# Feed-forward weight loads issued by SyncE in place of GpSimd, in a forward and backward kernel of one decode block

## The chip, the cores and the metric

The kernel runs on one core of a Trainium2 chip. The metric is device time in microseconds (us) of one execution. The kernel before was run three times: median 599.85 us, from 598.75 to 599.95. One further execution was recorded by the hardware profiler; it took 598.03 us, of which the profile shows a span of 596.2 us.

The core has five engines with their own instruction streams: TensorE (PE, with its weight loads PEld), VectorE (DVE), ScalarE (ACT), GpSimd (POOL) and SyncE (SP). A transfer between the chip's main memory and the on-chip memory is a DMA. An engine issues it and goes on; 16 DMA engines carry it out. DMAs issued by GpSimd go through queue q0 (its descriptors are written by software on GpSimd), those issued by SyncE through queue q1 (descriptors made by hardware). Instructions of one engine start in order: one that waits holds up all behind it on the same engine.

## The reference

One token with a model width of D = 1024 goes through a block of attention and a gated feed-forward layer, each with a layer norm that is scaled and shifted by a condition vector. The outputs are the result and the gradients of all inputs but one. Cut to what matters here:

```python
def _A_ref(x, k_cache, v_cache, wq, wo):       # attention over the last 4096 cache rows
    ...
def _B_ref(x, w_gate, w_up, w_down):           # D = 1024, F = 3584
    g = jnp.einsum('bsd,df->bsf', x, w_gate)
    u = jnp.einsum('bsd,df->bsf', x, w_up)
    h = _sigmoid(g) * u
    return jnp.einsum('bsf,fd->bsd', h, w_down)

mod = (_silu(c) @ w_mod).reshape(c.shape[0], 6, 1, -1)
h = _layernorm(x) * (1 + ca) + sa
x = x + ga * _A_ref(h, ...)
h = _layernorm(x) * (1 + cb) + sb
x = x + gb * _B_ref(h, ...)
_out, _vjp = jax.vjp(_f, A_x, A_k_cache, ...)  # and the gradients of grad_out
return (_out0, *grads)
```

There is one token, so each weight is used for one matrix-vector product forward and one backward, and its gradient is an outer product of two vectors, as large as the weight itself. The gradients of the two caches have 65,536 rows per head, of which all but the last 4,096 are zero; those zeros must be written too. That makes the kernel a mover of bytes: 60.30 MB are read from main memory and 185.60 MB are written.

## The kernel before

The stages follow each other: modulation vectors and query (to about 60 us), attention, a folding of the output projection into blocks (to about 300 us, TensorE work with `b_ps`), the feed-forward layer forward and backward in one sweep (about 310 to 480 us), and the remaining gradients (to the end). The instruction order on each engine is the order in which the program writes it; there is no planner.

Zeros are written by `zero(n)`: each call issues n fills of 1 MB on GpSimd (line 169; the "narrow" ones by lines 162 and 165). Their numbers at each point are given by hand in lists; for the feed-forward blocks this is `Z_FFN[q]`, four numbers for four places in a block, (1, 0, 0, 2) for blocks 0 to 4.

The feed-forward layer is cut into NB = 7 blocks of 512 columns of gate and up and 512 rows of down. A block's gate and up weights take 2 MB of the on-chip array `arena`, in one of two buffers (`q % 2`); each half (`j0` = 0 or 4, four groups of 128 rows of D) of each is a DMA of 512 KB, with four runs of 512 bf16 values (1 KB) in each partition. `load_ug` (line 863, its DMAs on line 865) loads, `store_ug` (line 867, DMAs on 869) stores the gradients, which are written over the weights in place. Down's weights have one buffer of 1 MB in two halves, loaded by `load_wd` (line 852) and stored by `store_wd` (line 855), both on SyncE, with one run of 4 KB per partition.

In the loop, iteration q does the following.

- Backward of block q: eight times a reduction on VectorE (`ttr`, line 210) over a weight slice and then its outer product, on ScalarE for the first five (line 241) and on VectorE for the other three (line 206), into the same bytes. After the fourth, `store_ug(q, 0, 4)` and `zero(z[0])`; after the eighth, `store_ug(q, 4, 4)` and `zero(z[1])`.
- Forward of block q + 1: `front` (64 products of 128 x 128 weight pieces on TensorE, line 954), `gates` (two sigmoids on ScalarE, line 959), `hh_ops` on VectorE, then in two halves `ffn_mm` (TensorE, line 971), `wd_ttr` and `wd_outer` (VectorE; `wd_outer` ends with `store_wd`), and `dug_part`, which prepares the vector for the next backward sweep.
- In between, `side()` runs transposes that later stages need, on TensorE and ScalarE.
- Loads of block q + 2 into the buffer that block q has left: `load_ug(q + 2, 0, 4)` after the first `wd_ttr`, `load_ug(q + 2, 4, 4)` after the second `wd_outer`, `zero(z[3])` behind it, and last `load_wd`.

A load waits until the stores of the same bytes have landed. All stores, fills and gate and up loads stand in GpSimd's one stream. The loads of blocks 0 and 1 are issued ahead of the loop.

Of the kernel before, what the change touches and what calls it, by code (L numbers as in the profile page):

```python
# [23 lines left out]
NB = F // FB  # L24
# [34 lines left out]
def kernel(  # L59
# [26 lines left out]
    nc = tc.nc  # L86
# [60 lines left out]
    def dep(later, earlier):  # L147
        tc.add_manual_dep(later.ins, earlier.ins.name,
                          mybir.DependencyInfo(mybir.DependencyClass.Sync, mybir.DependencyReason.DATA),
                          reason="pace")  # L150

    def zero(n, after=None):
        for _ in range(n):
            if len(zleft) <= keep[0]:
                return
            region, narrow_ = zleft.pop(0)
            first = None
            if narrow_:
                nc.gpsimd.inc_swdge_sem([], [], mode="reset_dge_cursor")  # L160
                n = nlen - ncount.pop()
                first = nc.gpsimd.dma_start(
                    out=rest[0:NS, 0:nlen * 128].rearrange("p (t x) -> p t x", t=2)[:, :, n * 64:(n + 1) * 64],
                    in_=zeros[0:NS, 0:64].rearrange("p (t x) -> p t x", t=1).broadcast_to([NS, 2, 64]))
                ins = nc.gpsimd.dma_start(
                    out=region[8:P, :].bitcast(FP32).rearrange("(t p) x -> p t x", t=2),
                    in_=zeros[0:60, :].rearrange("p (t x) -> p t x", t=1).broadcast_to([60, 2, ZW // 2]))
            else:
                ins = nc.gpsimd.dma_start(out=region.bitcast(FP32), in_=zeros[:, :])  # L169
            if after is not None:  # L170
                dep(first or ins, after)
# [26 lines left out]
    def addv(out, a, b):  # L198
        return tt(out, a, b, ALU.add)

    def cp(out, a):
        return nc.vector.tensor_copy(out=out, in_=a)  # L202
# [6 lines left out]
    def ttr(out, w, b, acc):  # L209
        return nc.vector.tensor_tensor_reduce(out=out, in0=w, in1=b, scale=1.0, scalar=0.0,  # L210
                                              op0=ALU.mult, op1=ALU.add, accum_out=acc)
# [233 lines left out]
    def side(n=1):  # L445
        for _ in range(n):
            if jobs:
                jobs.pop(0)()
# [402 lines left out]
    def load_wd(q, s):  # L851
        nc.sync.dma_start(out=wd_v[:, 2 * s:2 * s + 2, :], in_=wd_dram(B_w_down, q, s))
# [4 lines left out]
    def ug_part(view, q, j0, n):  # L857
        return view[:, j0:j0 + n, q * FB:(q + 1) * FB]

    def ug_tile(q, k, j0, n):  # L860
        return ug_v[:, q % 2, j0 // 4, j0 % 4:j0 % 4 + n, k, :]

    def load_ug(q, j0, n):
        for k, view in ((0, wu_view), (1, wg_view)):
            nc.gpsimd.dma_start(out=ug_tile(q, k, j0, n), in_=ug_part(view, q, j0, n))  # L865

    def store_ug(q, j0, n):
        for k, view in ((0, dwu_view), (1, dwg_view)):
            nc.gpsimd.dma_start(out=ug_part(view, q, j0, n), in_=ug_tile(q, k, j0, n))  # L869
# [20 lines left out]
    mod_tiles(md_ps, sb_t, range(4), True)  # L890
    wm_sec(5, 0, 4, 48)
    load_ug(0, 0, 4)
    load_ug(0, 4, 4)
    park(2, pna, "na")
    park(3, pna, "na")
# [29 lines left out]
    zero(Z_FOLD[0])  # L925
    park(4, ppq, "pq")
    load_ug(1, 0, 4)
    load_ug(1, 4, 4)
    zero(Z_FOLD[1])
# [18 lines left out]
    def front(q):  # L948
        gu = gu_t[q % 2]
        for col, k in ((4, 0), (0, 1)):  # L950
            for i in range(4):
                f0 = 256 * (i // 2) + i % 2
                for j in range(KD):
                    nc.tensor.matmul(gu[:, col + i:col + i + 1], lhsT=ug_v[:, q % 2, j // 4, j % 4, k, f0:f0 + 255:2],  # L954
                                     rhs=h2_bf[:, j:j + 1], start=(j == 0), stop=(j == KD - 1))

    def gates(q):
        r, gu = small[q % 2], gu_t[q % 2]
        nc.scalar.activation(out=r["sg"], in_=gu[:, 0:4], func=ACT.Sigmoid)
        nc.scalar.activation(out=r["om"], in_=gu[:, 0:4], func=ACT.Sigmoid, scale=-1.0)  # L960

    def hh_ops(q):
        r, up = small[q % 2], gu_t[q % 2][:, 4:8]
        mulv(r["hh_bf"], r["sg"], up)
        mulv(r["hh"], r["sg"], up)
        mulv(r["hom"], r["hh"], r["om"])

    def ffn_mm(q, s):
        for i in (2 * s, 2 * s + 1):
            for k in range(KD):  # L970
                nc.tensor.matmul(ffn_ps[:, k:k + 1], lhsT=wd_v[:, i, k * P:(k + 1) * P],
                                 rhs=small[q % 2]["hh_bf"][:, i:i + 1], start=(i == 0 and k == 0),
                                 stop=(i == 3), skip_group_check=True)

    def wd_ttr(q, s):
        for i in (2 * s, 2 * s + 1):
            ttr(junk, wd_v[:, i, :], b1k, small[q % 2]["dhh"][:, i:i + 1])

    def wd_outer(q, s):
        for i in (2 * s, 2 * s + 1):  # L980
            outer_dve(wd_v[:, i, :], small[q % 2]["hh"][:, i:i + 1], b1k)
        store_wd(q, s)

    def dug_part(q):
        r = small[q % 2]
        mulv(r["dug_bf"][:, 0:4], r["dhh"], r["sg"])
        mulv(r["dug_bf"][:, 4:8], r["dhh"], r["hom"])
        tp = new_tp("tp_dug")
        for i in range(8):
            nc.tensor.transpose(tp[:, i * P:(i + 1) * P], r["dug_bf"][:, i:i + 1].broadcast_to([P, P]), ident_bf[:, :])  # L990
        nc.scalar.copy(out=dug_b.rearrange("p (s f j) -> p s f j", s=4, j=2),  # L991
                       in_=tp.rearrange("p (s j f) -> p s f j", s=4, j=2))
# [6 lines left out]
    def unpark(p):  # L999
        nc.scalar.copy(out=B_home[p], in_=BT_ps[p][:, :])  # L1000
# [16 lines left out]
    for q in range(NB):  # L1017
        z = Z_FFN[q]
        more = q + 1 < NB
        for j in range(KD):  # L1020
            w = ug_v[:, q % 2, j // 4, j % 4, :, :].rearrange("p k f -> p (k f)")
            ttr(w, w, dug_b, dh2acc[:, q * KD + j:q * KD + j + 1])
            if not more and j in (3, 5, 6):
                unpark({3: 2, 5: 0, 6: 4}[j])
            (outer_act if j < 5 else outer_dve)(w, h2[:, j:j + 1], dug_b)
            if more and 0 < j < 5:
                side()
            if j == 0:
                if q == 0:
                    cp(ffn, ffn_ps)  # L1030
                else:
                    addv(ffn, ffn, ffn_ps)
            if j == 3:
                store_ug(q, 0, 4)
                zero(z[0])
        store_ug(q, 4, 4)
        zero(z[1])
        if more:
            front(q + 1)
            gates(q + 1)  # L1040
            side()
            hh_ops(q + 1)
            ffn_mm(q + 1, 0)
            wd_ttr(q + 1, 0)
            if q + 2 < NB:
                load_ug(q + 2, 0, 4)
            wd_outer(q + 1, 0)
            zero(z[2])
            side()
            ffn_mm(q + 1, 1)  # L1050
            wd_ttr(q + 1, 1)
            side()
            dug_part(q + 1)
            wd_outer(q + 1, 1)
            if q + 2 < NB:
                load_ug(q + 2, 4, 4)
            zero(z[3])
            if q + 2 < NB:
                load_wd(q + 2, 0)
                load_wd(q + 2, 1)  # L1060
        else:
            zero(z[2] + z[3])
# [270 lines left out]
```

## Time and profile before

| What | Value |
|---|---|
| Median of three runs | 599.85 us |
| The profiled execution's own time | 598.03 us |
| Its span in the profile | 596.2 us |
| Busy: TensorE / VectorE / ScalarE / GpSimd | 69% / 57% / 45% / 27% of the span |
| Moved by DMA | 246.63 MB, mean 414 GB/s |
| Zero fills of 1 MB | 114, median 16.2 us from issue to landing |
| Up and gate loads of 512 KB | 14 each, 9.4 and 9.6 us from issue to landing |
| Down loads and SyncE's stores of 512 KB | 14 and 20, 8.9 and 9.2 us |

How to read it: a page of the profile cuts the span into 40 slices of 14.9 us. In the row "DMA" a 9 means that the 16 engines had packets for 90% of the time or more; the row below gives GB/s. A table by window gives, for a stretch of the span, the busy time of each engine with its number of instructions, the granted TensorE clock, the DMA share (it can be over 1, as packets of two queues overlap in the records) and GB/s. A timeline row gives start, duration, engine, line, operation, what is written and read, and in brackets the idle time before and what ended it. A row of waits gives who waited for what: microseconds in total, how often, and the longest. Each transfer is carried out in packets, and the trace records start, size and duration of each packet and its queue.

### The profile page before, as it was taken

To read this page: it belongs to the slowest core of one execution; us is meant where nothing else is said; L and a number is where in the kernel's file an instruction comes from. 1 tells how busy PE (TensorE), PEld (TensorE's weight loads), DVE (VectorE), ACT (ScalarE), POOL (GpSimd) and SP (SyncE) were. 2 spreads that over 40 slices of the span, in tenths; PEclk is the share of its full clock that TensorE was granted. 3 is DMA by queue.
4 is the path that set the end of the run, shared out by engine and by line. 5 is a ranking of instruction groups with operands and counts; after the bars stand their busy time and mean duration, and the time that the engine had idled before them with its cause. 6 is when DMAs were issued, how large, how long until landed. Compare 5 with 4: busy or idle time off the path is not lost.

```text
span 596.2 us, 11043 instructions
## 1 busy us (share of the span) xinstructions
PE 409.2 (69%) x4587; PEld 275.6 (46%) x4612; DVE 337.7 (57%) x641; ACT 266.0 (45%) x408; POOL 159.4 (27%) x253
## 2 busy tenths in 40 slices
PE   3997688999999989999975436445445086774220
PEld 3995334334344545546654425434334066574220
DVE  3654499999511010070007587896787887858360
ACT  2589514567211014212224565773765835883110
POOL 3113123222222122222222224433423263223100
PEclk9999699999999999999995555555555586855555
DMA  8999999999999999999999999999999999999997
GB/s 348 421 417 420 413 425 417 426 425 424 429 420 424 421 430 422 423 423 423 422 399 412 420 387 414 404 405 409 403 410 408 420 420 413 422 423 426 424 426 326
DMA packets 45026, 246.63 MB, mean 414 GB/s; under 512 B 5085, under 2 KB 5085, under 8 KB 24544
## 3 DMA queue, kind: packets, MB, share of 16 engines
q0 software_dynamic: 37536, 217.60, 95.1%
q1 hardware_dynamic: 7392, 28.32, 13.1%
q8 instruction: 36, 0.59, 0.4%
q14 instruction: 14, 0.11, 0.0%
q10 hardware_dynamic: 48, 0.01, 0.0%
HBM read 60.30 MB, written 185.60 MB: 412 GB/s over the span
## 4 chain that ended last, share of the span: by engine, by line
DMA 38%; PE 32%; DVE 16%; ACT 5%; issue 4%; POOL 0%; DVEq 0%; ACTq 0%; POOLq 0%; SPq 0%
DMA out_dram<-arena 18%; PE b_ps L692 10%; DMA out_dram<-zeros 9%; PE n_ps L637 6%; DMA arena<-in_B_w_gate_dram 6%; DVE arena L206 5%; DMA arena<-in_B_w_down_dram 4%; DVE arena L193 4%; DVE junk L210 2%; PE t_ps L599 2%; DVE arena L210 2%; PE tp_wq L454 2%; PE w_ps L395 2%; PE tp_side L837 1%; PE tp_k L435 1%
## 5 line engine op out<-in xcount | busy, mean ns | idle before, releaser
L692 PE MATMUL b_ps<-arena 128*128 128x512 bf16 x494 | 113.4, 379 | 1.0 <-issue 0.2
L169 POOL DMA_DIRECT2D out_dram<-zeros x114 | 62.3, 548 | 178.7 <-DMA out_dram<-zeros 57.4
L837 PE MATMUL tp_side<-ident_bf,arena 128*128 128x128 bf16 x432 | 51.7, 300 | 48.1 <-ACT arena L838 41.2
L193 DVE TENSOR_TENSOR arena<-arena 128x2048 bf16<-128x2048 bf16 x64 | 76.5, 1223 | 2.3 <-PE n_ps L637 0.3
L692 PEld LDWEIGHTS <-arena 128*128 128x128 bf16 x512 | 48.7, 98 | 55.9 <-issue 2.9
L838 ACT COPY arena<-tp_side 128x1024 bf16<-128x1024 bf16 x54 | 54.0, 1012 | 42.7 <-PE tp_side L837 41.8
L210 DVE CUSTOM_DVE_ANT_0 arena<-arena,scr 128x1024 bf16<-128x1024 bf16 x56 | 66.2, 1220 | 9.9 <-ACT scr L991 9.9
L637 PE MATMUL n_ps<-arena 128*128 128x512 bf16 x249 | 65.1, 378 | 6.9 <-DVE arena L193 5.0
L837 PEld LDWEIGHTS <-arena 128*128 128x128 bf16 x432 | 43.4, 139 | 53.0 <-issue 52.6
L241 ACT ACTIVATE arena<-scr,h 128x1024 bf16<-128x1024 bf16 x35 | 40.1, 1149 | 9.6 <-DVE dh2acc L210 7.8
L637 PEld LDWEIGHTS <-arena 128*128 128x128 bf16 x256 | 24.6, 97 | 41.6 <-issue 16.2
L1162 ACT ACTIVATE arena<-ps_kv 128x512 bf16<-128x512 f32 x48 | 26.1, 680 | 30.4 <-PE ps_kv L1158 30.0
L202 DVE CAST arena<-b_ps 128x512 bf16<-128x512 f32 x6 | 4.2, 692 | 61.6 <-PE b_ps L692 61.6
L210 DVE CUSTOM_DVE_ANT_0 junk<-arena,b1k 128x1024 bf16<-128x1024 bf16 x28 | 34.2, 1222 | 6.8 <-DMA arena<-in_B_w_down_dram 6.3
L1158 PE MATMUL ps_kv<-junk,arena 8*128 8x128 bf16 x256 | 27.1, 303 | 13.9 <-DVE arena L206 12.6
L601 ACT CAST arena<-t_ps 128x512 bf16<-128x512 f32 x56 | 30.1, 589 | 12.1 <-PE t_ps L599 12.1
L869 POOL DMA_DIRECT2D out_dram<-arena x28 | 21.5, 772 | 42.6 <-ACT arena L241 32.1
L1158 PEld LDWEIGHTS <-arena 8*128 8x128 bf16 x256 | 25.2, 140 | 15.6 <-issue 15.6
L456 ACT COPY arena<-tp_wq 128x1024 bf16<-128x1024 bf16 x23 | 21.7, 1041 | 7.9 <-PE tp_wq L454 7.9
L865 POOL DMA_DIRECT2D arena<-in_B_w_up_dram x14 | 10.6, 755 | 48.1 <-DMA out_dram<-arena 24.8
L954 PE MATMUL fg<-h_bf,arena 128*128 128x1 bf16 x448 | 14.7, 166 | 11.5 <-DMA arena<-in_B_w_gate_dram 8.7
L206 DVE TENSOR_SCALAR arena<-arena,cs_col 128x4096 bf16<-128x4096 bf16 (+1 forms) x16 | 16.1, 1020 | 10.3 <-DMA out_dram<-arena 10.2
(302 smaller groups left out, 639.5 us busy)
## 6 DMA issues: line engine op xcount, KB each, us to landing
out_dram<-zeros POOLq DMA_DIRECT2D x114, 1024.0 KB, 16.2
out_dram<-arena POOLq DMA_DIRECT2D x27, 1024.0 KB, 19.0
out_dram<-arena POOLq DMA_DIRECT2D x30, 512.0 KB, 11.9
out_dram<-arena SPq DMA_DIRECT2D x20, 512.0 KB, 9.2
arena<-in_A_wq_dram POOLq DMA_DIRECT2D x8, 1024.0 KB, 20.7
arena<-in_A_wo_dram POOLq DMA_DIRECT2D x8, 1024.0 KB, 12.5
arena<-in_w_mod_dram POOLq DMA_DIRECT2D x7, 1024.0 KB, 18.2
arena<-in_B_w_down_dram SPq DMA_DIRECT2D x14, 512.0 KB, 8.9
```

The source lines that it names most:

```text
L169: ins = nc.gpsimd.dma_start(out=region.bitcast(FP32), in_=zeros[:, :])
L193: return nc.vector.tensor_tensor(out=out, in0=a, in1=b, op=op)
L206: return nc.vector.tensor_scalar(out=out, in0=a, scalar1=s1, scalar2=None, op0=op0)
L210: return nc.vector.tensor_tensor_reduce(out=out, in0=w, in1=b, scale=1.0, scalar=0.0, op0=ALU.mult, op1=ALU.add, accum_out=acc)
L241: return nc.scalar.activation(out=out, in_=b, func=ACT.Copy, scale=col)
L601: nc.scalar.copy(out=o, in_=ps)
L637: mm = nc.tensor.matmul(nbank[k][:, :], lhsT=k_nat[:, g, t_ * DH:(t_ + 1) * DH], rhs=vp[:, t_ % 2, 4 * k:4 * k + 4, :].rearrange("p h d -> ...
L692: mm = nc.tensor.matmul(bbank[p][k][:, :], lhsT=a4[:, p, h, :], rhs=wo_t[u][:, a, k * 512:(k + 1) * 512], start=(i == 0 and a == 0), stop= ...
L837: nc.tensor.transpose(tp[:, i * P:(i + 1) * P], blk[:, i * P:(i + 1) * P], ident_bf[:, :])
L838: nc.scalar.copy(out=blk if dst is None else dst, in_=tp[:, :])
L1158: nc.tensor.matmul(ps[:, t4 * DH:(t4 + 1) * DH], lhsT=rows[32 * g:32 * g + HG, t_ * P:(t_ + 1) * P], rhs=hd[32 * g:32 * g + HG, :], start= ...
L1162: nc.scalar.activation(out=o, in_=ps[:, :], func=ACT.Copy, scale=float(scale))
```

## The change

`load_ug` gets a parameter for the issuing engine. The loads of blocks 0 and 1 stay with GpSimd; those of blocks 2 to 6, which are issued inside the loop, go to SyncE, and both of their calls stand earlier in the program: the first half right after `store_ug(q, 4, 4)` and `zero(z[1])`, ahead of `front(q + 1)`; the second half between the two `wd_outer` calls. On TensorE, VectorE and ScalarE the order of the instructions is the same as before. GpSimd's stream loses 20 DMAs; what is left there keeps its order. On SyncE a block's order is now: up and gate first half, `store_wd` 0, up and gate second half, `store_wd` 1, the two `load_wd`.

```diff
-    def load_ug(q, j0, n):
+    def load_ug(q, j0, n, eng=nc.gpsimd):
         for k, view in ((0, wu_view), (1, wg_view)):
-            nc.gpsimd.dma_start(out=ug_tile(q, k, j0, n), in_=ug_part(view, q, j0, n))
+            eng.dma_start(out=ug_tile(q, k, j0, n), in_=ug_part(view, q, j0, n))
...
         store_ug(q, 4, 4)
         zero(z[1])
         if more:
+            if q + 2 < NB:
+                load_ug(q + 2, 0, 4, nc.sync)
             front(q + 1)
             gates(q + 1)
             side()
             hh_ops(q + 1)
             ffn_mm(q + 1, 0)
             wd_ttr(q + 1, 0)
-            if q + 2 < NB:
-                load_ug(q + 2, 0, 4)
             wd_outer(q + 1, 0)
             zero(z[2])
+            if q + 2 < NB:
+                load_ug(q + 2, 4, 4, nc.sync)
             side()
             ffn_mm(q + 1, 1)
             wd_ttr(q + 1, 1)
             side()
             dug_part(q + 1)
             wd_outer(q + 1, 1)
-            if q + 2 < NB:
-                load_ug(q + 2, 4, 4)
             zero(z[3])
             if q + 2 < NB:
                 load_wd(q + 2, 0)
                 load_wd(q + 2, 1)
```

## The prediction

> **What bounds the kernel now.** I read the page first for its DMA lines, then long windows of the trace by stage, then the waits and the order of time around one feed-forward block.
>
> ```profile
> DMA  8999999999999999999999999999999999999997
> GB/s 348 421 417 420 413 425 417 426 425 424 429 420 424 421 430 422 423 423 423 422 399 412 420 387 414 404 405 409 403 410 408 420 420 413 422 423 426 424 426 326
> q0 software_dynamic: 37536, 217.60, 95.1%
> q1 hardware_dynamic: 7392, 28.32, 13.1%
> ```
>
> From the first slice to the last the 16 DMA engines are busy; the shares of the two queues even add to more than 100%, because packets of two queues overlap in the records. 246.63 MB at 414 GB/s is the whole span of 596.2 us. So an edit counts only if it changes the rate, or leaves the engines without work. Slices 21 to 31 (about 300 to 460 us) are the slowest.
>
> ```profile
> 310.00:358.00 48.00, 20.95 (x320) 18.27 (x317) 33.35 (x70) 24.70 (x28) 12.74 (x19) 0.51 1.11 408
> 358.00:449.00 91.00, 43.19 (x642) 37.59 (x640) 72.61 (x149) 55.09 (x62) 32.44 (x47) 0.50 1.08 407
> 471.00:550.00 79.00, 52.75 (x824) 43.55 (x825) 60.19 (x144) 47.45 (x79) 29.36 (x38) 0.65 1.08 421
> 550.00:590.00 40.00, 8.17 (x74) 7.36 (x72) 16.14 (x23) 5.76 (x10) 3.28 (x5) 0.50 1.01 425
> ```
>
> The last two numbers are the DMA share and GB/s. The feed-forward stage runs at 407, the end at 421 to 425, without a hole; the last DMA is issued at 577 us and the rest is draining. What the feed-forward stage wins or loses in DMA time therefore reaches the end in full.
>
> Inside a block (times from 422 us):
>
> ```profile
> 422.14 0.75 POOL L865 DMA_DIRECT2D arena<-in_B_w_gate_dram  x1 [1.77 <-DMA out_dram<-arena]
> 422.88 1.11 POOL L169 DMA_DIRECT2D out_dram<-zeros  x2
> 426.44 1.54 POOL L869 DMA_DIRECT2D out_dram<-arena  x2 [2.45 <-ACT arena L241]
> 427.97 0.60 POOL L162 DMA_DIRECT2D out_dram<-zeros  x1
> 428.56 0.68 POOL L165 DMA_DIRECT2D out_dram<-zeros  x1
> 430.05 1.57 POOL L869 DMA_DIRECT2D out_dram<-arena  x2 [0.81 <-ACT arena L838]
> 430.44 1.65 PEld L954 LDWEIGHTS <-arena 128*128 128x128 bf16 x59 [2.15 <-DMA arena<-in_B_w_gate_dram]
> 437.45 0.76 POOL L865 DMA_DIRECT2D arena<-in_B_w_up_dram  x1 [5.84 <-PE tp_side L837]
> ```
>
> The loads of a block wait on GpSimd for the stores of the same buffer, and hold two zero fills behind them; those fills then stand in the queue ahead of the next stores. The stores issued at 426.44 let the load of their bytes go only at 437.45, 11 us later. TensorE's front waits for the last gate load, and the gates behind it:
>
> ```profile
> POOL arena L865 <- DMA out_dram<-arena: 33.7, 13, 6.5
> ACT sg L959 <- PE fg L954: 19.2, 7, 5.6
> DVE hh_bf L193 <- ACT om L960: 19.1, 7, 5.4
> ```
>
> So there is a compute wait of some 3 us in most blocks (3.0 at 429.5), but under it the DMA share stays above 1. It is a symptom of the bound, and is not itself the bound.
>
> **What the skill says.** The Trainium skill, DMA: Bandwidth & Descriptors, "Issuing engines are not separate DMA queues", states that DMAs of all issuers share the 16 engines, so that another issuer saves only the sequencer's time. This trace agrees: with both queues loaded (428 to 430 us) the rate is 418 GB/s, no higher than the 420 to 430 of the slices in which GpSimd's queue runs alone. That says the move gains no bandwidth. The same page, "Why small descriptors are slow", puts a fixed overhead on every packet. The trace agrees here too. The median durations of the packet records on SyncE's queue are 18 ns for 256 bytes, 84 for 2,048, 161 for 4,096 and 309 for 8,192: a line of 8 to 9 ns plus bytes at 27.2 per ns ((8,192 - 256) / (309 - 18) = 27.3). I go by this line. The page's "SWDGE descriptor pipeline" lets GpSimd's generator fill packets up to 4,096 bytes, and GpSimd's records agree: a gate or up row is four runs of 1 KB, and those loads show as 4,096-byte packets. For SyncE's hardware generator, "Why a DMA increments its semaphore by 16" says a descriptor is one contiguous run; whether four runs become one packet no DMA here shows, since all of SyncE's transfers have one run per partition.
>
> **The change part by part.** Twenty DMAs of 512 KB move (five blocks, two halves, up and gate), 10.49 MB.
>
> GpSimd loses 20 x 0.755 us = 15.1 us of descriptor writing and the waits for stores. It is 27% busy: nothing on the path. The two zero fills go out right after the second stores, near T+5.2 (T is the issue of a block's first stores) in place of T+19.4. The next stores find the queue drained: they land near T+4 in place of T+11.
>
> SyncE gains 20 issues. Its present issue takes 0.34 us for 128 rows; for four times the runs I allow 0.34 to 1.4 us, so 6.8 to 28 us over 115 us on an engine with nothing else to do: nothing, unless it makes the next DMA late. Behind a waiting load stand, in order, the first w_down store (ready at T+9.7), the second half of the loads, the second w_down store (T+12.6) and the two w_down loads. The first loads are ready at about T+4 and T+5, the second near T+11: the w_down stores are held by at most some 2 us at issue.
>
> The engines serve the queues in turn by packets, 4,096 against 8,192 bytes now. If SyncE's are 1,024 bytes, it gets a ninth of the bandwidth beside zero fills and a fifth beside stores. By hand: GpSimd's 5.2 MB of a block take until about T+15; by then 0.6 MB of the loads are in; the rest of the loads, and w_down's stores ahead of and behind them, end near T+22, the w_down loads at T+24.5 and T+26.5. Front needs the up and gate loads at T+25 to T+26, ffn_mm its w_down at T+27 to T+28. So nothing starves, with 2 to 4 us to spare, and the engines have work throughout.
>
> The compute wait of about 16 us over the six gates mostly goes. I cost this at nothing: with it gone a block would need 20.3 us of compute, but its 9.44 MB take 22.8 us of DMA time (96 packets of 4,096 bytes per engine x 160 ns = 15.4, and 24 of 8,192 x 308 = 7.4, where 308 ns is 8,192 x 16 / 425 GB/s, the rate of fills alone). What is late next is the DMA itself, as before.
>
> What remains is DMA time. Gain: from 358 to 449 us the records hold 6,011 packets of 4,096 bytes and 1,509 of 8,192; at 160 and 308 ns over 16 engines that is 60.1 + 29.0 = 89.2 of 91 us. The 2 us left, and about 0.5 in the block before, are the stretches where only loads run (373 GB/s at 424 to 426 us, where up and gate loads meet w_down loads). Loads spread among stores and fills can win 0 to 2.5 us; I take 1.3. Loss: with 1,024-byte packets at 37.6 + 8.6 = 46.3 ns, 10,240 packets over 16 engines take 29.6 us in place of 2,560 x 160 / 16 = 25.6: +4.0 us. With merged packets the loss is 0; the skill's fixed 3 cycles, 32 bytes a cycle, would make it 7% (35 cycles x 4 against 131), 1.8 us. I take 3.8, as the line through four sizes is measured here. The sum: 598.03 - 1.3 + 3.8 = 600.5 in the profiled execution's own terms (span 596.2 and 1.8 around it). The median of the runs is 1.8 above that execution, so 602.3.
>
> **Rivals.** (A, the forecast) Split packets cost DMA time: 602.3, its own range 600.5 to 604. For it: the bound is DMA time and the durations lie on a line. Against: merging is not shown either way, and overlap between the queues (shares up to 1.2 for a stretch) may hide some overhead.
>
> (B, the other side) The hardware queue merges the four runs, or overlap hides them, and only the early release remains: 599.85 less 1.3 to 2.5, so 598. For it: loads at the head of their own queue, no fills in front of stores. Its place is 345 to 460 us; it decides if an up or gate packet on SyncE costs at most 41 ns per KB, against 46.
>
> (C) Both effects are about equal, or zero: 599.9. A transfer hidden anyway, conserved bytes, the same end. For it: the end stage runs at 424 whatever comes before.
>
> (D) SyncE's order and the unequal turns make the w_down loads or the second loads late: past T+28 or T+26 the compute waits again, longer than now. At 1 us more in each of five blocks, with the engines short of work, that adds to A: 607. Against it: 2 to 4 us of slack by the working above, and bytes still waiting in the queues.
>
> **How the numbers follow.** A 0.52, B 0.24, C 0.14, D 0.10. A measurement tells 0.2%, 1.2 us, from no change. Slower takes most of A (0.49), all of D: 0.59. Faster takes most of B and a little of C: 0.24. The same: 0.17. The range goes from 598.0, the middle of B, to 605.0, between A and D.
>
> **What would show it.** On SyncE's queue: bytes 28.3 + 10.5 = 38.8 MB, and in case A 7,680 packets more than with merging (about 18,000 in all, against 10,300 with merged ones). The rate from 358 to 449 us falls below 407 in A (about 400), rises to 412 or more in B. The gates' wait should shrink from 19 us to 8 or less in both; in D the waits on w_down grow in its place. The page's GpSimd share falls by 15 us, with no effect. I am wrong if packets are split and the stage is still not longer (overhead hidden), or if DMA slices below 9 appear in the stage.

## The result, and the profile after

The changed kernel takes 606.67 us (median of four runs, 604.3 to 607.4) against 599.75 us of the kernel before (median of four here): 6.9 us slower. The recorded ratio is 1.0105, 95% interval 1.0083 to 1.0128 (the quotient of the medians would be 1.0115). The forecast was 602.3 us with a range up to 605.0: the direction was right, the size and the range were not. The profiled execution took 606.2 us, with a span of 604.4 us.

The first fence is the page's DMA part of the changed kernel: busy tenths and GB/s in 40 slices, then packets, MB and share of the 16 engines for each queue.

```profile
DMA  9999999999999999999999999999998999999997
GB/s 350 418 418 421 414 425 418 427 424 427 426 421 425 424 426 421 426 424 425 419 402 409 412 383 363 400 401 360 402 410 307 420 420 415 420 421 425 425 427 323
q0 software_dynamic: 34656, 207.11, 89.1%
q1 hardware_dynamic: 17952, 38.81, 18.2%
```

SyncE's queue q1 has 10.5 MB and 10,560 packets more. Of these, 10,240 are of 1,024 bytes, with a median of 46 ns in the records (mean 50.8): the hardware queue does not merge the four runs of a partition. That is the split of case A, which had 46.3 ns. But one slice moves only 307 GB/s, and 1 KB packets of 46.3 ns alone would still give 354 on 16 engines. That slice also falls below 9 in the DMA row, which the prediction had named as a sign of being wrong. By stage (last two numbers: DMA share and GB/s):

```profile
310.00:358.00 48.00, 21.12 (x338) 18.65 (x336) 30.87 (x67) 22.15 (x26) 9.12 (x14) 0.53 1.14 410
358.00:449.00 91.00, 38.77 (x599) 33.66 (x596) 63.56 (x131) 49.00 (x55) 20.26 (x30) 0.50 1.07 387
449.00:471.00 22.00, 11.16 (x179) 10.08 (x180) 18.21 (x38) 13.66 (x15) 5.82 (x9) 0.50 0.93 335
471.00:550.00 79.00, 49.68 (x782) 39.76 (x779) 64.74 (x151) 51.48 (x79) 25.18 (x35) 0.63 1.07 420
```

The stretch from 449 to 471 us in the kernel before, for comparison:

```profile
449.00:471.00 22.00, 7.76 (x136) 6.90 (x135) 16.75 (x36) 12.74 (x15) 5.70 (x10) 0.50 1.15 414
```

From 471 to 550 us the rate, 420, is the same as before (421); the loss lies between 358 and 471 us (387 in place of 407, then 335 in place of 414). Finer windows show its form, here around the stores of two blocks (4 us each, the last of 1 us):

```profile
408.00:412.00 4.00, 1.80 (x17) 1.48 (x15) 3.93 (x8) 3.90 (x5) 0.84 (x2) 0.50 0.96 368
412.00:416.00 4.00, 3.95 (x96) 3.85 (x96) 3.01 (x8) 2.64 (x5) 2.63 (x4) 0.50 0.89 256
416.00:420.00 4.00, 1.97 (x30) 1.70 (x30) 3.55 (x7) 1.61 (x2) 1.20 (x3) 0.50 1.09 410
460.00:464.00 4.00, 1.80 (x17) 1.48 (x15) 3.93 (x8) 3.90 (x5) 0.83 (x2) 0.50 0.52 181
464.00:468.00 4.00, 3.96 (x96) 3.86 (x96) 3.01 (x8) 2.64 (x5) 2.64 (x4) 0.50 0.89 308
461.00:462.00 1.00, 0.12 (x2) 0.12 (x2) 1.00 (x3) 1.00 (x2) 0.00 (x0) 0.50 0.09 37
```

For some microseconds of some blocks the DMA engines have too little to do (a share of 0.52 and 181 GB/s over 4 us, 0.09 and 37 GB/s in the worst one). VectorE (third column) is fully busy in the same windows: the sweep of the block is running late, and its stores, which would feed the engines, are not issued yet. The waits say what made it late; first the kernel before, then the changed one:

```profile
PEld L971 <- DMA arena<-in_B_w_down_dram: 10.5, 5, 5.1
DVE junk L210 <- DMA arena<-in_B_w_down_dram: 6.3, 3, 5.0
```

```profile
PEld L971 <- DMA arena<-in_B_w_down_dram: 28.3, 8, 6.3
DVE junk L210 <- DMA arena<-in_B_w_down_dram: 19.0, 8, 4.3
ACT sg L959 <- PE fg L954: 12.7, 7, 5.8
```

TensorE's weight load for `ffn_mm` (line 971) waits 28.3 us for w_down in place of 10.5; VectorE's `wd_ttr` (line 210, `junk`) waits 19.0 in place of 6.3. The wait for the gates fell from 19.2 to 12.7 us, so the early release of the gate and up loads works. It has been exchanged for a later w_down. One block in the timeline: GpSimd's and SyncE's issues, and the two halves of TensorE's w_down weight loads; other rows are left out:

```profile
384.46 1.54 POOL L869 DMA_DIRECT2D out_dram<-arena  x2 [16.56 <-ACT arena L241]
384.69 4.38 SPq L852 DMA_DIRECT2D arena<-in_B_w_down_dram  x2
389.40 1.11 POOL L169 DMA_DIRECT2D out_dram<-zeros  x2
390.73 0.51 PEld L971 LDWEIGHTS <-arena 128*128 128x128 bf16 x16 [0.93 <-DMA arena<-in_B_w_down_dram]
391.19 0.38 SPq L865 DMA_DIRECT2D arena<-in_B_w_up_dram  x1
394.03 0.75 SPq L855 DMA_DIRECT2D out_dram<-arena  x1
397.92 0.37 SPq L865 DMA_DIRECT2D arena<-in_B_w_up_dram  x1
398.28 0.50 PEld L971 LDWEIGHTS <-arena 128*128 128x128 bf16 x16 [6.35 <-DMA arena<-in_B_w_down_dram]
399.57 0.37 SPq L865 DMA_DIRECT2D arena<-in_B_w_gate_dram  x1
401.85 1.84 SPq L855 DMA_DIRECT2D out_dram<-arena  x1
408.36 0.34 SPq L852 DMA_DIRECT2D arena<-in_B_w_down_dram  x1
```

T, the issue of the block's first gate and up stores, is 384.46. The first w_down store is issued at 394.03 (T+9.6), as soon as its data is ready, and its load only at 408.36 (T+23.9): the store needed 14 us to land, with split loads in front of it in its queue. The median time from issue to landing of the w_down stores (line 855), before and then after:

```profile
DMA to landing us min/median/max: 8.1/8.4/9.7
DMA to landing us min/median/max: 9.3/13.6/14.2
```

Over the blocks in the middle the first w_down load went out at T+16.7 to T+20.0 before and at T+22.3 to T+25.5 after, the second some 2.5 us behind it before and 4 to 7 us after.

To separate the price of packets from empty engines I add up the packet records at fixed prices, 46.3, 84, 160 and 308 ns for 1, 2, 4 and 8 KB over 16 engines (the few other sizes by the prediction's line, instruction fetches left out). Before, they are worth 588.4 of the 596.2 us, so 7.9 us are left over; after, 592.4 of 604.4, so 12.0. Of the 8.2 us of longer span, 4.0 are the packets at list price, and 4.1 are time in which the engines did less than they could. This is an accounting at assumed prices, not a measurement of either part, and of one execution each.

### The profile page after: what moved, and what is told of

Its sections match the earlier page's. It is cut to its first block, busy times and chain, and to the rows that moved or that the text cites. A ratio compares the mean times of both kernels' runs of the same rounds, so it can differ in the third digit from the quotient of the medians.

```text
span 604.4 us, 11087 instructions
## 1 busy us (share of the span) xinstructions
PE 413.5 (68%) x4612; PEld 277.0 (46%) x4612; DVE 337.4 (56%) x641; ACT 266.1 (44%) x408; POOL 140.5 (23%) x233
## 4 chain that ended last, share of the span: by engine, by line
PE 36%; DMA 33%; DVE 17%; ACT 6%; issue 4%; POOL 0%; DVEq 0%; ACTq 0%; SPq 0%; POOLq 0%
DMA out_dram<-arena 17%; PE b_ps L692 13%; DMA arena<-in_B_w_down_dram 7%; PE n_ps L637 6%; DMA arena<-in_w_mod_dram 5%; DVE arena L206 4%; DMA out_dram<-zeros 4%; DVE arena L193 4%; DVE junk L210 3%; DVE arena L210 3%; PE t_ps L599 2%; PE w_ps L395 2%; PE tp_wq L454 2%; PE fold_ps L876 1%; PE tp_side L837 1%
## 5 line engine op out<-in xcount | busy, mean ns | idle before, releaser
L692 PE MATMUL b_ps<-arena 128*128 128x512 bf16 x512 | 119.1, 386 | 0.0
L692 PEld LDWEIGHTS <-arena 128*128 128x128 bf16 x512 | 49.6, 100 | 57.9 <-issue 6.8
L837 PEld LDWEIGHTS <-arena 128*128 128x128 bf16 x432 | 43.0, 138 | 50.6 <-issue 50.3
L637 PEld LDWEIGHTS <-arena 128*128 128x128 bf16 x256 | 24.6, 97 | 41.6 <-issue 16.2
L1158 PE MATMUL ps_kv<-junk,arena 8*128 8x128 bf16 x256 | 27.3, 305 | 15.4 <-DVE arena L206 14.3
L971 PE MATMUL fg<-hh_bf,arena 128*128 128x1 bf16 x224 | 8.3, 167 | 26.8 <-DMA arena<-in_B_w_down_dram 26.1
L971 PEld LDWEIGHTS <-arena 128*128 128x128 bf16 x224 | 7.4, 106 | 29.1 <-DMA arena<-in_B_w_down_dram 28.3
## 6 DMA issues: line engine op xcount, KB each, us to landing
out_dram<-arena SPq DMA_DIRECT2D x20, 512.0 KB, 13.6
```

Source lines behind the costliest of these rows:

```text
L637: mm = nc.tensor.matmul(nbank[k][:, :], lhsT=k_nat[:, g, t_ * DH:(t_ + 1) * DH], rhs=vp[:, t_ % 2, 4 * k:4 * k + 4, :].rearrange("p h d -> ...
L692: mm = nc.tensor.matmul(bbank[p][k][:, :], lhsT=a4[:, p, h, :], rhs=wo_t[u][:, a, k * 512:(k + 1) * 512], start=(i == 0 and a == 0), stop= ...
L837: nc.tensor.transpose(tp[:, i * P:(i + 1) * P], blk[:, i * P:(i + 1) * P], ident_bf[:, :])
L1158: nc.tensor.matmul(ps[:, t4 * DH:(t4 + 1) * DH], lhsT=rows[32 * g:32 * g + HG, t_ * P:(t_ + 1) * P], rhs=hd[32 * g:32 * g + HG, :], start= ...
```

## The experiments

The questions: is the price of split packets real (theory P), and what makes w_down late (theory W): the small packets' share of the turns, the fills that now go out early, or the place of w_down's transfers behind the loads in SyncE's queue? Ratios are to the kernel before on the same chip. "Left over" is the sum above, from each run's profile; the wait is that of TensorE's weight load for w_down (line 971 of the changed kernel; before: 10.5 us). Both come from one profiled execution, which lies up to 4.0 us from its kernel's median (e8), so a difference of one or two us in "left over" says little.

| Kernel | Median us | Before us | Ratio (95% interval) | Left over us | w_down wait us |
|---|---|---|---|---|---|
| changed kernel | 606.67 | 599.75 | 1.0105 (1.0083 to 1.0128) | 12.0 | 28.3 |
| e1: runs of 4 KB | 603.70 | 599.82 | 1.0063 (1.0035 to 1.0091) | 12.8 | 24.0 |
| e2: late fills | 600.52 | 599.82 | 1.0008 (0.9984 to 1.0031) | 7.3 | 27.3 |
| e3: store first | 599.45 | 599.82 | 0.9989 (0.9974 to 1.0005) | 4.0 | 13.3 |
| e4: before, early fills | 601.73 | 599.82 | 1.0031 (1.0018 to 1.0043) | 12.2 | 6.7 |
| e5: store first, 4 KB | 596.50 | 599.23 | 0.9950 (0.9932 to 0.9968) | 7.0 | 13.0 |
| e6: store first, late fills | 599.07 | 599.23 | 1.0006 (0.9992 to 1.0020) | 4.1 | 13.2 |
| e7: changed kernel again | 607.50 | 599.23 | 1.0120 (1.0083 to 1.0157) | 13.1 | 31.4 |
| e8: late fills, 4 KB | 608.41 | 599.23 | 1.0146 (1.0115 to 1.0177) | 14.2 | 26.6 |
| e9: w_down on GpSimd | 602.00 | 599.15 | 1.0036 (1.0018 to 1.0055) | 7.6 | 6.9 |
| e10: half of e3's order | 600.32 | 599.15 | 1.0028 (1.0014 to 1.0043) | 6.4 | 13.9 |

### e1: SyncE's loads in runs of 4 KB

```diff
+    def load_ug_4k(q, j0):
+        for i, view in ((0, wu_view), (1, wg_view)):
+            nc.sync.dma_start(out=ug_v[:, q % 2, j0 // 4, 2 * i:2 * i + 2, :, :].rearrange("p j k f -> p (j k f)"),
+                              in_=view[:, j0, min(q * FB, F - 4 * FB):min(q * FB, F - 4 * FB) + 4 * FB])
...
-                load_ug(q + 2, 0, 4, nc.sync)
+                load_ug_4k(q + 2, 0)
...
-                load_ug(q + 2, 4, 4, nc.sync)
+                load_ug_4k(q + 2, 4)
```

> The changed kernel, but SyncE's twenty loads read runs of 4 KB in place of 1 KB: same number and size of DMAs, same buffer in total, other values of the same two matrices (so the feed-forward values of blocks 2 to 6 are not the reference's). Theory P (split packets cost 4.0 us of DMA time) and theory W (w_down is late and the engines run dry, 4 us). If small packets also cause W, through their smaller share in the turns of the queues: both go, 598 to 600, w_down waits back to some 10 us. If W comes from the order in SyncE's queue or from the early fills alone: only P goes, 602.5, and the waits on w_down stay at 25 us or more. If P is wrong: 606.

603.70, ratio 1.0063. The packets' worth falls back to 588.4, and 3.0 us go; the wait on w_down stays at 24.0 and the time left over at 12.8. The w_down stores still take 12.2 us to land. So split packets have a price, but their smaller share of the turns is not, or not mainly, what makes w_down late. (Each load here covers parts of both up and gate, so it waits for both stores; and it reads other addresses, so what is called the price of split packets may hold more than the packets.)

### e2: the changed kernel with late fills

```diff
-            (outer_act if j < 5 else outer_dve)(w, h2[:, j:j + 1], dug_b)
+            o_ins = (outer_act if j < 5 else outer_dve)(w, h2[:, j:j + 1], dug_b)
+            if q and j == 1:
+                zero(Z_FFN[q - 1][3], o_ins)
...
-            zero(z[3])
```

> The changed kernel, but the two fills at the end of a block are issued after the second outer product of the next block's sweep, about where they were before the change (some 18 us after the block's first stores). If W comes from the early fills (they take the turns while the loads are wanted, and are gone when w_down is waited for): the lost time goes, P stays: 602 to 603. If W comes from the order in SyncE's queue: 606 to 607. P alone predicts that packet time stays at 4 us above before.

600.52, below what was expected of either theory, with w_down as late as ever (27.3 us). So a late w_down alone does not make the loss: in this kernel the loss is gone although the wait for w_down is as long as in the changed kernel. It looked as if the fills merely covered the wait. e8 below shows that this was not a general cover.

### e3: the w_down store ahead of each half

```diff
         if more:
-            if q + 2 < NB:
-                load_ug(q + 2, 0, 4, nc.sync)
             front(q + 1)
...
             wd_outer(q + 1, 0)
             zero(z[2])
             if q + 2 < NB:
-                load_ug(q + 2, 4, 4, nc.sync)
+                load_ug(q + 2, 0, 4, nc.sync)
...
             wd_outer(q + 1, 1)
+            if q + 2 < NB:
+                load_ug(q + 2, 4, 4, nc.sync)
             zero(z[3])
```

> The changed kernel, but SyncE issues each w_down store ahead of a half of the loads: store 0, first half, store 1, second half, then the w_down loads. If W comes from w_down's stores standing behind 1 MB of split loads in one queue: w_down loads are issued earlier (some 14 us after the stores of the block in place of 24), waits on w_down fall to some 10 us, 602.5. If it comes from the small packets' share of turns or the early fills: 605 to 608, since the w_down loads still stand behind all loads.

599.45, ratio 0.9989, 3 us below what was expected, which gave back only the 4.1 us of time in which the engines did less (the time left over fell by 8.0, from 12.0 to 4.0): the whole loss is gone, with the same packets (10,240 of 1 KB), the same early fills and loads issued later. The w_down loads go out at 401.48 for stores at 381.82 (T+19.7; expected was some T+14) in place of T+23.9. Waits and windows of this kernel:

```profile
PEld L971 <- DMA arena<-in_B_w_down_dram: 13.3, 8, 5.8
DVE junk L210 <- DMA arena<-in_B_w_down_dram: 6.9, 4, 5.6
ACT sg L959 <- PE fg L954: 22.2, 7, 5.5
358.00:449.00 91.00, 41.71 (x628) 36.34 (x628) 68.83 (x144) 51.82 (x58) 20.26 (x30) 0.50 1.10 403
449.00:471.00 22.00, 9.63 (x151) 8.09 (x149) 16.26 (x34) 12.01 (x14) 5.73 (x9) 0.50 1.14 413
```

The waits on w_down are halved and more, that for the gates is back at 22.2 and costs nothing, since the engines have work under it (403 and 413 GB/s in place of 387 and 335). In these runs a wait is dear where little else is queued.

### e4: the kernel before with early fills

```diff
         zero(z[1])
         if more:
+            zero(z[3])
             front(q + 1)
...
-            zero(z[3])
```

> The kernel before (loads on GpSimd) with the two fills of a block's end moved ahead of the block's loads, as they come to stand in the changed kernel. If early fills alone leave the engines dry: slower than before by 2 to 4 us, 602 to 604. If W needs the loads in SyncE's queue: 599 to 601, the same as before or up to 1 us faster, as stores no longer stand behind fills.

601.73, ratio 1.0031: 1.9 us slower, on the edge of what was expected if early fills alone matter. Here it is the gates that wait (27.1 us), not w_down (6.7), presumably because the loads stand behind the fills in GpSimd's queue. So the early place of the fills has a cost of its own on GpSimd's queue; in e3 the same place costs nothing visible.

### e5: store first, with runs of 4 KB

The edits of e3 and e1 together.

> The order of the store-first kernel with SyncE's twenty loads in runs of 4 KB (other values of the same matrices in blocks 2 to 6). With the late w_down mended, only the price of the split packets is taken away here. Theory P at the full 4.0 us: 4 us below the store-first kernel, 595.5. If half of that price is hidden by overlap of the two queues: 597.5. If all of it is hidden: 599.5, the same.

596.50, ratio 0.9950. Against e3's 0.9989 that is 0.39%, by the medians 2.4 us: the price of the split packets, in place of 4.0. The two intervals leave 0.9 to 3.8 us for it. The rest of the list price is hidden: e3 has 4.0 us left over, e5 7.0 (a rough split, as the profiled execution lies 1.2 us below the median in e3 and 0.7 above it in e5). With the packets merged and w_down in time, the loads on SyncE win 2.7 us. The window of the stage:

```profile
358.00:449.00 91.00, 42.66 (x636) 37.29 (x635) 70.51 (x147) 53.53 (x60) 20.28 (x30) 0.50 1.10 413
```

That is 413 against 407 before. It is no version to use, because its runs of 4 KB are not the weights that the block needs.

### e6: store first and late fills

The edits of e3 and e2 together.

> Both mendings: store-first order and late fills, split packets as in the changed kernel. If late w_down costs time only where no fills are left to cover it, one mending is enough and the second adds little: 599 to 600. If the two losses were separate and additive (7.3 by order, 6.2 by fills out of 6.9): far below before, 594 to 596. A measurement below 598.6 would be a version better than both.

599.07, ratio 1.0006: one mending is enough, the second adds nothing. It is the same as before within the measurement, and no version was found that beats both kernels.

### e7: the changed kernel again

No edit.

> The changed kernel itself, beside the others on this chip, so that differences to it are taken on one chip: 606 to 607, and 6 to 7 us above before, if the chip makes no difference.

607.50, 8.3 us above before on this chip, a little more than expected; the interval overlaps that of the first measurement. Again the w_down wait is 31.4 us and the engines fall dry (13.1 us left over).

### e8: late fills with runs of 4 KB

The edits of e1 and e2 together.

> The changed kernel with late fills and runs of 4 KB on SyncE (other values of the same matrices in blocks 2 to 6), w_down still behind all loads. If the price of split packets is 4.0 us and fills cover the late w_down: 596.5. If overlap hides half: 598.5. If 600 or above: the cover by late fills is incomplete, and the price of packets is hidden in waiting time that stays.

608.41: no expectation held, since it is not 600 but slower than the changed kernel. Two of its dips:

```profile
400.00:404.00 4.00, 1.01 (x8) 0.85 (x8) 3.24 (x6) 2.63 (x3) 0.00 (x0) 0.50 0.97 288
404.00:408.00 4.00, 1.55 (x14) 1.39 (x14) 3.96 (x9) 3.95 (x5) 1.10 (x2) 0.50 1.07 422
452.00:456.00 4.00, 1.01 (x8) 0.85 (x8) 3.78 (x8) 2.63 (x4) 0.00 (x0) 0.50 0.82 283
456.00:460.00 4.00, 2.02 (x16) 1.70 (x16) 3.96 (x8) 3.89 (x5) 1.09 (x2) 0.50 1.02 346
```

They end about when the held fills go out (at 404.69 and 456.15, two fills in the fifth column). The fills are tied to the sweep, the sweep waits for w_down, and here the loads are done before: the engines run short ahead of the fills. In e2 the slow split loads reached about as far as the fills. So late fills are no cover against a late w_down in general; they were in e2 by timing. This reading fits the windows, but was not tested further.

### e9: w_down on GpSimd

```diff
-        nc.sync.dma_start(out=wd_v[...], in_=wd_dram(B_w_down, q, s))
+        (nc.gpsimd if q > 1 else nc.sync).dma_start(out=wd_v[...], in_=wd_dram(B_w_down, q, s))
...
-        nc.sync.dma_start(out=wd_dram(out_8, q, s), in_=wd_v[...])
+        (nc.gpsimd if q else nc.sync).dma_start(out=wd_dram(out_8, q, s), in_=wd_v[...])
...
+            zero(z[3])
             wd_outer(q + 1, 0)
...
-            zero(z[3])
```

> The changed kernel with its loads on SyncE issued at the same places and its early fills, but w_down's stores (from block 1) and loads (from block 2) are issued by GpSimd, behind the fills, so that they don't stand behind split loads in SyncE's queue. Theory W (w_down is late because of its place behind the loads in one queue): waits on w_down fall from 28 us to 13 or less, 599 to 601. If the early fills or GpSimd's waits make them late just as well: waits stay above 20 us, 604 or more.

602.00, ratio 1.0036. With loads and fills as early as in the changed kernel, taking w_down out of the loads' queue brings its wait to 6.9 us and the left-over time to 7.6. The time is 1 us above the expected band: now the gates wait 27.1 us, presumably because w_down's transfers, in 4 KB packets on the other queue, take turns from the split loads.

### e10: half of the order

```diff
             zero(z[2])
-            if q + 2 < NB:
-                load_ug(q + 2, 4, 4, nc.sync)
...
             wd_outer(q + 1, 1)
+            if q + 2 < NB:
+                load_ug(q + 2, 4, 4, nc.sync)
             zero(z[3])
```

> The changed kernel with one step towards the store-first order: the second half of the loads goes behind the second w_down store; the first half stays early, ahead of the first store. Theory W, place in the queue: store 0 is still behind the first half, the w_down loads behind the second half, so about half of the loss goes: 602 to 604. If only the first half ahead of store 0 matters: 606 to 607; if only the second half ahead of store 1: 599 to 600.

600.32, ratio 1.0028, near the third case. Store 0 still stands behind the first half, and the first w_down load goes out as late as in the changed kernel (429.75 for stores at 405.19, T+24.6). But both w_down loads now go together, 1.5 us for the pair; in the changed kernel the second followed after 4 us, near T+28. So the second half ahead of store 1 makes most of the loss; expected was about half.

## Why the prediction was wrong

- **The bound.** Right. DMA time is the limit, the stage after is untouched (420 against 421 GB/s), and what the feed-forward stage lost arrived at the end in full.
- **Split packets.** Right in mechanism: not merged, 46 ns each. As a term of the sum it was 3.8 us and measured 2.4 (e5 against e3, 0.9 to 3.8 by the intervals; 3.0 between e1 and the changed kernel). The estimate from the skill's 3 cycles a packet (DMA: Bandwidth & Descriptors, "Why small descriptors are slow") had been 1.8 us; the measurement can't tell it from 2.4, and reaches the 3.8 only at its edge. That the two queues together hide part of what single durations show is argued, not shown. Nor is the price a constant: with late fills, merged packets made the kernel slower (e8 against e2).
- **Early release of the loads.** Right in sign; I took 1.3 us of at most 2.5, and it is 2.7 where nothing spoils it (e5 against before, though e5 issues the loads later than the changed kernel does).
- **"So nothing starves, with 2 to 4 us to spare".** This is the step that failed. I had the w_down loads done at T+24.5 and T+26.5. In the block above they were only issued at T+23.9 and T+27.9. For the block before it, with T at 362.44, the weight load that wanted the second half got it at 398.28, T+35.8, after 6.35 us of waiting. What I had too short was the landing of the w_down stores: 13.6 us in place of the 8.4 before. They were held at issue by no more than 2.3 us (once 4.2), about what I had allowed.
- **What lay under that step.** Two numbers were wrong. The second half's loads were to go near T+11 and went at T+13.5 and T+15.1 (T+12 to T+17 over the blocks). And GpSimd's bytes were to be gone by T+15: its records last to about T+20, and until then the split loads crawl (between 399 and 402.5 us, fills 360 GB/s, the 1 KB packets 50), with w_down's store behind them. The first stores were to land near T+4; the first load went at T+3.8 and T+4.1 in two blocks and at T+6.7 and T+9.6 in two others, and w_down was late in all four, so this is not what decides. I had worked one block out from empty queues, and at T the w_down loads of the block before were only starting (384.69 beside 384.46). How one block acts on the next stays open: the blocks took 22.0, 26.7, 20.8 and 31.2 us in turn, so the lateness does not simply grow.
- **"I cost this at nothing"** (the compute wait that goes). That wait did shrink, but another took its place, and its cover, the DMA backlog, was gone for some microseconds. That a wait costs nothing fits the kernel before, where the engines had work under the waits; here the w_down round trip, store, landing and load, was at times almost the only transfer left.
- **The rivals.** Forecast A and rival D came together: split packets (+2.4), early release (-2.7), w_down late with early fills (+7.3, from e3 to the changed kernel). They add to the 6.9 measured because they are successive differences of the same times, so the sum is no test. Two things were luck. The direction came right through D and not through A: without the late w_down (e3) the change is worth -0.4 us, inside its interval. And D, with a chance of 0.10, had the time, 607, but as 2.5 + 5 where the runs give -0.3 + 7.3. What I said against D, slack and waiting bytes, was the working that failed. D has a condition that I did not see: in e2 w_down is as late and the loss is gone.
- **Readings.** Counted by their starts, the packets from 358 to 449 us are 6,083 of 4,096 bytes and 1,464 of 8,192, worth 89.0 us; the 2 us left over stand. GpSimd's queue also has 19,792 packets of 8,192 bytes, so the 4,096 that the prediction gives its generator are no upper limit here.

## What to carry to other kernels

When loads move to another queue, work out what stands behind them in that queue over two blocks, not one, starting with what the block before leaves there; here a store-then-load round trip on a single buffer had to go ahead of bulk loads. DMA engines that are never idle hide waits; before a change that reorders transfers, ask of each wait what else would be queued during it. Count packets by their contiguous runs: on SyncE's queue the same bytes cost some 2.4 us more in 1 KB runs than in 4 KB runs.

## What the runs showed of the hardware

- SyncE's queue makes one packet of each 1 KB run (10,240 packets, 46 ns), where GpSimd's makes one of 4,096 bytes of four runs (160 ns). Beside 8 KB fills (399 to 402.5 us of the changed kernel) the 1 KB packets got 50 GB/s to 360, nearly the ratio of the packet sizes. Their median duration there was 88 ns, nearly double.
- An issue on SyncE can itself take longer behind split loads: w_down's stores took 0.34 us each before and up to 3.1 us after (median 0.55). It is a guess, not shown, that the queue had no room.
